# Attention and channel mix in one kernel: the gate by tanh, batch 1 mixed by differences, attention denominators by DVE turns, PSUM banks by name, and a new order of the work

## The chip, the cores and the metric

The kernel runs on one core of a Trainium2 chip. The metric is device time in microseconds (us). A core has five engines with queues of their own: TensorE (PE) for matmuls and transposes into PSUM, VectorE (DVE), ScalarE (ACT), GpSimd (POOL) and SyncE (SP). Here POOL issues the loads, SP the stores, and ACT the first load and the last stores. Before the change the kernel takes 203.44 us, the median of 3 runs (202.97 to 203.64).

## The reference

For each of 8 batches and 8 heads, with 576 tokens, heads of 64 and 32 memory slots:

```python
a = exp(phi - max(phi, axis=2)); a = a / sum(a, axis=2)      # over the tokens
k_m = einsum('bhsm,bhsd->bhmd', a, k); v_m = einsum('bhsm,bhsd->bhmd', a, v)
attn = softmax(scale * q @ k_m.T)                            # over 32 slots
x = (attn @ v_m), heads side by side                         # 8 x 576 x 512
xk = mu_k * x + (1 - mu_k) * x_prev; xr = mu_r * x + (1 - mu_r) * x_prev
k = relu(xk @ w_k); v = (k * k) @ w_v; r = 1 / (1 + exp(-(xr @ w_r)))
out = r * v
```

x_prev is x one token earlier, with zeros ahead of the first. The channel mix has 1024 inner channels. Outputs are float32; inside, most tiles are bfloat16.

## The kernel before, in words

The order of all work is written out in PLAN, a list of words. A word `2:x0` is step x0 of batch 2; `c1:5` is block 5 of the keys of token chunk 1; `g:7` is the gate of token tile 7; `o:7` its value product and store; `sg:3` settles the gates of tiles 6 and 7; `p:` words issue loads. Each engine goes through its own instructions in this order and waits where a semaphore tells it to. A step that waits therefore holds up all that stands behind it on its engine.

A batch's attention goes through these steps:
- `exp` (ACT): the exponential of phi. `z` (PE, L246, then a reciprocal on DVE): its sums. `kv`, or `k` and `v` apart (PE, L236): the sums over the tokens, 72 small matmuls that run several at a time in parts of the array.
- `nk` or `ak`: K scaled by 1/sum, on DVE or ACT. `tk`: turned by PE, copied from PSUM. `q0`, `q1`: q turned on DVE (L323). `s`: scores on PE (L338) and their exponentials on ACT (L343).
- The denominators of the second softmax come in one of two ways. By PE: `l0` to `l3` (L353) sum the 32 slots by a matmul with ones, ACT takes the logarithm (L358) and the exponential of its negative (`h.z`, `r.z`, L363). By turns: `fe` turns the exponentials on DVE, `fs` sums and inverts them, `fo` turns the result back. Batches 0, 1 and 3 go by PE, the others by turns.
- `y` or `w` (DVE, L387): weights times inverse denominators.
- The values and the mixing with the token before also come in two ways. By PE: `nk0` ... `nr1` scale V by 1/sum and by mu or 1 - mu, and `mk0`, `mk1`, `mr0`, `mr1` (L292) add both products in PSUM; ACT and DVE copy xk and xr out (L450). By differences: `x0`, `x1` (L292, copied by ACT, L399) give x, `dd` subtracts the token before on DVE (L411), `k0d` ... `r2e` scale the difference by mu - 1 on DVE or ACT (L424, L422) and add x on DVE (L425). Batches 0 and 1 are mixed by PE, the others by differences.

The channel mix works on chunks of tokens: chunk 0 is batch 0 in two halves (320 and 256 tokens), the others have 512 tokens. A key block is 4 matmuls (L526), a Relu on ACT (L531) and a square on DVE (L540). A gate is 4 matmuls (L556) and exp(-x) on ACT (L561); settling takes the logarithm of 1 + that and the exponential of its negative, for two tiles at once (L567, L568). A value product is 8 matmuls (L582), a product with the gate on DVE (L584), and stores.

Matmuls on a tile of zeros whose result nobody reads (`busy`, L192) stand at two places at the start, 16 of 512 columns.

POOL loads q, k, v and phi of a batch, batch 0 by halves of 64 partitions, and the weights wk, wr, wv in parts; the loads turn float32 into bfloat16, but for phi. PSUM has eight banks, used in turn by one tag with eight buffers.

Of the kernel before, what the change touches and what calls it, by code (L numbers as in the profile page):

```python
# [19 lines left out]
    "0:busy10 0:exp1 0:mub 0:exp0 p:k:0b 0:k0c 0:z 0:hn0 0:k1c p:q:0a 0:ht0 p:q:0b 0:hn1 p:v:0b 0:hc1 0:qh0 0:qh1",  # L20
    "p:v:0a 0:s0 0:l1 0:h1z 0:l0 0:mu 0:s1 0:y1 0:v1c 0:v0c 0:nk1 p:wk:0-4 0:nr0 p:wr:0-4 p:wk:4-8 0:nk0 0:l3 0:h0z",
    "0:y0 0:l2 0:h3z 0:h2z 0:busy6 0:y3 0:y2 0:nr1 0:mr1 0:mk0 g:3 0:mk1 c0:2a 0:mr0 c0:0a p:phi:1 1:exp 7:load p:k:1",
    "c0:4a c0:1a g:2 c0:0b c0:6a 1:z c0:5a p:q:1 c0:1b 1:k 1:nk sg:1 g:0 6:load 1:q0 1:tk 1:q1 c0:4b c0:5b g:1 c0:7b",
    "c0:2b 1:s p:v:1 c0:7a c0:3b c0:3a c0:6b 1:l2 1:v 1:nk1 1:nr1 1:nk0 p:wv:0-2 1:l1 1:l3 1:nr0 1:h2z 1:h1z 1:l0",
    "1:y2 1:y1 1:h3z p:wv:2-4 0:load 1:load 1:y3 1:h0z 1:y0 o:2a o:3a 1:mk1 1:mk0 1:mr0 2:exp c1:5 c1:0 c1:7 1:mr1",
    "c1:3 2:z c1:1 c1:4 o:3b sg:0 2:kv 2:nk o:2b 2:tk 2:q0 2:q1 c1:2 c1:6 o:1b 2:s 2:nv o:1a 3:exp 2:fe g:5 g:4 2:fs",
    "2:fo 2:w0 3:z sg:2 2:w1 o:0b o:4 o:5 2:x0 3:kv 3:nk g:7 3:nv 3:q0 2:x1 g:6 2:load 3:tk 3:q1 2:dd o:0a sg:3 2:k0d",
    "g:8 3:s 4:exp 2:k2d o:6 o:7 3:l1 3:l3 3:l2 2:r0d 3:l0 c2:4 3:r0z 3:w0 3:r1z 3:w1 c2:1 c2:3 3:load c2:0 c2:7 c2:2",
    "4:z 2:r2d 3:x1 4:q0 c2:5 c2:6 3:x0 4:kv 3:dd 4:q1 4:ak 3:k2d g:9 sg:4 o:8 4:tk o:9 3:k0d 4:av 5:exp g:12 g:11",
    "g:10 5:z 4:s 3:r2d 5:kv 3:r0d 4:fe 5:q0 sg:5 c3:2 5:q1 c3:1 c3:7 4:fs 5:av c3:5 g:13 4:fo 5:load 4:load c3:6",  # L30
    "4:w0 7:exp 4:w1 5:ak c3:4 c3:3 o:10 sg:6 o:11 c3:0 7:q1 4:x1 g:14 g:15 7:z 4:x0 sg:7 7:q0 5:tk 4:dd o:12 o:15",
    "6:exp 7:kv 7:ak 5:s 7:av 4:k2d 4:k0d o:14 5:fe 7:tk 4:r2e 6:z o:13 5:fs c4:3 4:r0e 5:fo c4:4 5:w1 c4:5 6:kv 7:s",
    "6:av 6:ak 5:w0 6:q1 6:q0 c4:6 c4:1 g:19 7:fe c4:2 g:16 g:17 5:x0 c4:0 6:tk c4:7 7:fs 5:x1 sg:8 5:dd g:18 sg:9",
    "o:17 5:k0d 5:k2d 6:s o:16 o:19 o:18 5:r2e 5:r0e c5:5 6:fe c5:1 g:21 c5:2 g:20 6:fs c5:0 6:fo sg:10 6:w0 6:w1",
    "c5:3 g:23 c5:4 c5:6 g:22 c5:7 7:fo 6:x1 o:20 7:w0 7:w1 6:x0 sg:11 6:dd o:21 o:22 7:x0 g:25 6:k0d g:24 6:k2d 7:x1",
    "sg:12 7:dd o:23 7:k0d g:26 7:k2d c6:0 6:r0e c6:1 c6:4 6:r2e c6:7 c6:3 c6:5 c6:2 c6:6 c7:4 7:r0e c7:2 c7:7 c7:3",
    "g:27 7:r2e c7:6 c7:0 sg:13 c7:1 o:26 o:25 c7:5 o:27 g:29 o:24 c8:1 c8:4 g:31 g:28 c8:3 sg:14 c8:6 c8:7 g:30 c8:5",
    "o:28 o:29 sg:15 c8:2 o:30 o:31 c8:0 g:33 g:32 sg:16 g:35 g:34 o:33 o:32 sg:17 o:34 o:35",
# [4 lines left out]
SUMS = ()  # L43


NJ = 9


@with_exitstack
def kernel(  # L50
# [13 lines left out]
    nc = tc.nc  # L64
# [18 lines left out]
    ld = ctx.enter_context(tc.sbuf_pool(name="ld", bufs=2))  # L83
    work = ctx.enter_context(tc.sbuf_pool(name="work", bufs=2))
    psum = ctx.enter_context(tc.psum_pool(name="psum", bufs=1))


# [14 lines left out]
    def load_phi(b, eng):  # L102
        ph = ld.tile([128, HH, NJ, M], F32, name="ph", tag="ph")
        eng.dma_start(out=ph.rearrange("p h j m -> p h (j m)"), in_=rows(phi[b]))
        loads[b] = ph
# [25 lines left out]
    nc.scalar.preload_act_table_set("natural_log_exp_and_others")  # L131
# [9 lines left out]
    def preload(word):  # L141
# [6 lines left out]
        elif what == "id":  # L148
            make_identity(nc, identity)
        else:  # L150
            n = int(part[0])
            if what == "phi":
                load_phi(n, nc.gpsimd)
            else:
                dst = qs[n].rearrange("p (h j) d -> p h j d", j=NJ) if what == "q" else kvs[n][:, "kv".index(what)]
                src = {"q": q, "k": k, "v": v}[what][n]
                if n:
                    load_rows(dst, src)
                else:
                    load_parity(dst, src, ROWS["ab".index(part[1])])  # L160

    for word in PRE.split():
        preload(word)

# [23 lines left out]
    def keep_busy(n, blocks=CT // 128):  # L188

        ps = psum.tile([128, CT], F32, name="idle", tag="ps", bufs=8)[:, :blocks * 128]  # L190
# [5 lines left out]
    def load_mu_b():  # L196
        ps = psum.tile([128, 2, 2, D], F32, name="mub", tag="ps", bufs=8)
# [7 lines left out]
    def load_mu():  # L205
        ps_mu = psum.tile([128, 2 * ND], F32, name="psmu", tag="ps", bufs=8)
        nc.tensor.transpose(ps_mu, mu2, ident_f)
        nc.vector.tensor_scalar_add(mu1, ps_mu, -1.0)

    def attention(b):  # L210
        st = {}

        def ps_tile(shape, dtype, name):
            return psum.tile(shape, dtype, name=name, tag="ps", bufs=8)
# [27 lines left out]
        def esum():  # L242
            st["zps"] = ps_tile([128, 2], F32, "zps")
            parts = [em[:, j].rearrange("p h m -> p (h m)") for j in range(NJ)] if b not in SUMS else st["es"]
            for i, part in enumerate(parts):
                nc.tensor.matmul(st["zps"], lhsT=part, rhs=ones, start=i == 0, stop=i == len(parts) - 1,  # L246
                                 skip_group_check=True)
            st["rz"] = work.tile([128, 2], F32, name="rz", tag="rz", bufs=3)
            nc.vector.reciprocal(st["rz"], st["zps"])

        def sum_rows():

            left = work.tile([128, HH * M], F32, name="es", tag="es", bufs=1)
            nc.vector.reduce_sum(left, em.rearrange("p j h m -> p (h m) j"), axis=mybir.AxisListType.X)
            terms = work.tile([128, 3, HH * M], BF16, name="et", tag="et", bufs=1)
            for i in range(3):
                nc.vector.tensor_copy(terms[:, i], left)
                if i < 2:
                    nc.vector.tensor_sub(left, left, terms[:, i])
            st["es"] = [terms[:, i] for i in range(3)]  # L260

        def norm_k(cs=(0, 1), by_act=False):

            def go():
                if "kbd" not in st:
                    st["kbd"] = work.tile([128, 2, 2, 2, PB], BF16, name="kbd", tag="kbd", bufs=3)
# [9 lines left out]
        def norm_v(by_act=False):  # L276

            def go():
                vb = work.tile([128, 2, D], BF16, name="vb", tag="vb", bufs=3)
# [19 lines left out]
        def tr_k(cs=(0, 1), copy=nc.vector.tensor_copy):  # L299

            def go():
# [6 lines left out]
                if "kmT" not in st:  # L308
                    st["kmT"] = work.tile([128, 2, 128], BF16, name="kmT", tag="kmT", bufs=3)
# [3 lines left out]
        def q_tile():  # L313
            if "qT" not in st:
                st["qT"] = work.tile([128, HH, NJ * PB, 2], BF16, name="qT", tag="qT", bufs=2)
# [10 lines left out]
        def scores(cs):  # L326

            def go():
                if "e" not in st:
                    st["e"] = work.tile([128, 2, S], BF16, name="e", tag="e", bufs=3)  # L330
# [15 lines left out]
        def denom(c, hf, by_dve=False):  # L346

            def go():
                if "lz" not in st:
                    st["lz"] = work.tile([128, 2, S], F32, name="lz", tag="lz", bufs=2)  # L350
# [15 lines left out]
        def fold_e():  # L366
            eT = work.tile([128, 2 * NJ, M, 2], BF16, name="eT", tag="eT", bufs=1)
            nc.vector.transpose(eT.rearrange("p b m h -> p (b m h)").bitcast(U32),
                                st["e"].rearrange("p c s -> p (c s)").bitcast(U32))
# [269 lines left out]
```

## Time and profile before

| | |
|---|---|
| median of 3 runs | 203.44 us |
| span of the profiled execution | 201.9 us |
| mean granted PE clock | 0.975 |
| busy: PE, DVE, ACT, POOL | 191.1, 147.1, 156.9, 29.3 us |
| matmuls: keys, values, gates | 352, 328, 144 |
| settling the gates on ACT | 19.4 + 19.0 us |
| squares of the keys on DVE | 31.4 us |
| DMA moved | 31.29 MB, mean 155 GB/s |

The result file holds no time of the profiled execution itself beside its span; the span runs from its first to its last instruction, so what lies around it is the difference from the times, 1.5 us from the median.

A profile line gives an engine's line in the kernel, the operation, the tile written and those read, the shape and the count, the busy us and the mean ns of one, and the idle time ahead of it with what ended that. In the row of slices, each digit is the busy share of 5 us in tenths. A line of a timeline gives the start, the length of a merged run of equal instructions, and in brackets the engine's wait before it. Busy times of matmuls overlap, so times on PE are best read from one start to the next.

### The profile page before, as it was taken

Reading aid. Unit: us, or ns where it says so; the run is one execution under the profiler, and the core shown is the slowest. Engines: PE = TensorE matmul, PEld = TensorE weight load, DVE = VectorE, ACT = ScalarE, POOL = GpSimd, SP = SyncE. Lnnn points to the kernel's source line nnn. Section 1 sums busy time; section 2 is a strip of 40 time slices with the busy share of each in tenths; the row PEclk is TensorE's granted clock in tenths of the full one; section 3 lists DMA queues with packets and bytes.
Section 4 is the critical chain, followed back from the end, with each engine's and each line's share of the span. In section 5 each row is a group of like instructions: output and inputs, shape, how many; then the busy total and the mean of one; then the engine's idle time right before and its main releaser. Section 6 shows DMA issues by size and latency. Waiting matters only on the chain.

```text
span 201.9 us, 5395 instructions
## 1 busy us (share of the span) xinstructions
PE 191.1 (95%) x2179; PEld 98.4 (49%) x2179; DVE 147.1 (73%) x347; ACT 156.9 (78%) x313; POOL 29.3 (15%) x45
## 2 busy tenths in 40 slices
PE   8459999899999999999999999999999999999992
PEld 2324576546654445544456654444444444444451
DVE  2366566967898989999699979998998835243231
ACT  3146899787858989899896999988999992592760
POOL 7743412212204100045000000000000000000000
PEclk9856999999999999999999999999999999999999
DMA  6999999999999999989999200520242004404435
GB/s 161 167 204 209 264 208 198 265 223 270 222 265 258 236 311 210 288 149 205 247 247 271 66 3 17 123 67 3 65 95 54 3 0 107 101 0 107 104 71 136
DMA packets 24521, 31.29 MB, mean 155 GB/s; under 512 B 1960, under 2 KB 19632, under 8 KB 24496
## 3 DMA queue, kind: packets, MB, share of 16 engines
q0 software_dynamic: 17392, 20.91, 55.6%
q1 hardware_dynamic: 6336, 9.18, 17.4%
q10 hardware_dynamic: 768, 0.85, 1.3%
q8 instruction: 17, 0.28, 0.5%
q14 instruction: 8, 0.07, 0.1%
HBM read 38.28 MB, written 9.44 MB: 236 GB/s over the span
## 4 chain that ended last, share of the span: by engine, by line
PE 90%; DMA 4%; ACT 2%; DVE 1%; POOL 1%; issue 1%; POOLq 0%
PE pk L526 31%; PE pv L582 30%; PE pr L556 16%; DMA q<-in_q_dram 4%; PE kvps L236 4%; PE scps L338 2%; PE mxps L292 2%; PE nops L292 2%; PE idle L192 1%; PE zps L353 1%; PE zps L246 1%; DVE qT L323 1%; POOL kv L111 1%; ACT lz L358 0%; ACT lz L363 0%
## 5 line engine op out<-in xcount | busy, mean ns | idle before, releaser
L526 PE MATMUL pk<-xkT,wk 128*128 128x512 bf16 (+4 forms) x352 | 67.9, 341 | 0.0
L582 PE MATMUL pv<-wv,sq 128*128 128x512 bf16 (+1 forms) x328 | 66.4, 353 | 0.4 <-ACT lz L358 0.4
L531 ACT ACTIVATE rl<-pk 128x512 bf16<-128x512 f32 (+3 forms) x80 | 41.4, 566 | 13.7 <-PE pk L526 12.8
L526 PEld LDWEIGHTS <-wk 128*128 128x128 bf16 x352 | 32.9, 98 | 28.7 <-issue 0.8
L582 PEld LDWEIGHTS <-sq 128*128 128x128 bf16 x328 | 31.1, 98 | 30.3 <-issue 0.8
L540 DVE TENSOR_TENSOR sq<-rl 128x512 bf16<-128x512 bf16 (+5 forms) x104 | 31.4, 334 | 19.2 <-ACT rl L531 18.7
L556 PE MATMUL pr<-wr,xrT 128*128 128x512 bf16 x144 | 35.4, 379 | 0.5 <-ACT xrT L450 0.5
L584 DVE TENSOR_TENSOR o<-sg,pv 128x512 f32<-128x512 f32 (+1 forms) x41 | 24.6, 617 | 13.3 <-PE pv L582 13.1
L561 ACT ACTIVATE sg<-pr 128x512 f32<-128x512 f32 x36 | 21.4, 610 | 5.6 <-PE pr L556 4.8
L556 PEld LDWEIGHTS <-xrT 128*128 128x128 bf16 x144 | 13.4, 98 | 15.2 <-ACT xrT L450 0.6
L567 ACT ACTIVATE sg<-sg 128x1024 f32<-128x1024 f32 x18 | 19.4, 1079 | 0.2
L568 ACT ACTIVATE sg<-sg 128x1024 f32<-128x1024 f32 x18 | 19.0, 1058 | 0.6
L399 ACT CAST x<-nops 128x320 bf16<-128x320 f32 (+1 forms) x48 | 15.7, 426 | 3.2 <-PE nops L292 3.2
L323 DVE STREAM_TRANSPOSE qT<-q 128x576 uint32<-128x576 uint32 (+1 forms) x16 | 13.3, 839 | 2.2 <-DMA q<-in_q_dram 2.1
L387 DVE TENSOR_TENSOR atn<-e,lz 128x576 bf16<-128x576 bf16 (+2 forms) x20 | 12.1, 633 | 1.1 <-ACT lz L363 0.7
L343 ACT ACTIVATE e<-scps 128x288 bf16<-128x288 f32 x32 | 10.6, 416 | 2.5 <-PE scps L338 2.3
L422 ACT ACTIVATE mu_d<-diff,mu 128x576 bf16<-128x576 bf16 x16 | 11.6, 797 | 0.2 <-DVE xkT L425 0.2
L224 ACT ACTIVATE em<-ph 128x1152 bf16<-128x1152 f32 (+1 forms) x9 | 9.4, 1060 | 2.6 <-DMA ph<-in_phi_dram 2.6
L425 DVE TENSOR_TENSOR xrT<-x,mu_d 128x1152 bf16<-128x1152 bf16 x12 | 9.1, 755 | 3.2 <-ACT mu_d L422 3.0
L236 PE MATMUL kvps<-kv,em 64*32 64x128 bf16 (+1 forms) x720 | 8.8, 217 | 2.1 <-DMA kv<-in_k_dram 2.1
L424 DVE TENSOR_SCALAR mu_d<-diff,mu 128x576 bf16<-128x576 bf16 x32 | 10.2, 363 | 0.0
L108 POOL DMA_DIRECT2D kv<-in_k_dram x7 | 5.2, 746 | 32.1 <-PE kvps L236 26.4
(66 smaller groups left out, 152.6 us busy)
## 6 DMA issues: line engine op xcount, KB each, us to landing
out_dram<-o SPq DMA_DIRECT2D x61, 128.0 KB, 2.4
ph<-in_phi_dram POOLq DMA_DIRECT2D x7, 576.0 KB, 19.5
kv<-in_k_dram POOLq DMA_DIRECT2D x7, 576.0 KB, 18.7
q<-in_q_dram POOLq DMA_DIRECT2D x7, 576.0 KB, 21.2
kv<-in_v_dram POOLq DMA_DIRECT2D x7, 576.0 KB, 20.8
out_dram<-o SPq DMA_DIRECT2D x18, 64.0 KB, 5.3
wk<-in_moe_w_k_dram POOLq DMA_DIRECT2D x2, 512.0 KB, 13.6
wv<-in_moe_w_v_dram POOLq DMA_DIRECT2D x2, 512.0 KB, 20.5
```

The source lines that it names most:

```text
L236: nc.tensor.matmul(kvps[c][g * M:(g + 1) * M], lhsT=em[ROWS[c], j, g, :], rhs=kv5[ROWS[c], parts, g, j, :], start=j == 0, stop=j == NJ - 1 ...
L323: nc.vector.transpose(dst.bitcast(U32), src.bitcast(U32))
L399: nc.scalar.copy(st["x"][:, i, sl], pss[i])
L526: nc.tensor.matmul(pk[:, p0 - lo:p1 - lo], lhsT=wk_sb[:, di, fi * 128:(fi + 1) * 128], rhs=xk_T[:, di, p0 % RING:p0 % RING + p1 - p0], sta ...
L531: nc.scalar.activation(rl, pk, AF.Relu)
L540: nc.vector.tensor_mul(sq[:, fi, p:p + p1 - p0], rl[:, part], rl[:, part])
L556: nc.tensor.matmul(pr, lhsT=xr_T[:, di, c0:c0 + 128], rhs=wr_sb[:, di, :], start=(di == 0), stop=(di == ND - 1))
L561: nc.scalar.activation(sg[:, t % 2], pr, AF.Exp, scale=-1.0)
L567: nc.scalar.activation(gated[p], gated[p], AF.Ln, bias=1.0)
L568: nc.scalar.activation(gated[p], gated[p], AF.Exp, scale=-1.0)
L582: nc.tensor.matmul(pv[:, cols], lhsT=sq[:, fi, p:p + 128], rhs=wv_sb[:, fi, cols], start=(fi == 0), stop=(fi == NF - 1))
L584: nc.vector.tensor_mul(o[:, cols], gated[t // 2][:, t % 2, cols], pv[:, cols])
```

## The change

It has these parts:
- The gate: r = 1/(1 + exp(-z)) becomes (1 + tanh(z/2))/2. ACT does one Tanh for a tile, settling goes, and DVE's product becomes (tanh + 1) times the value in one scalar_tensor_tensor. The half is put into the keys: Relu scales by the root of 1/2. The instruction list shows a second load of an ACT table ahead of the first Tanh; the first load stands behind the issue of the first K load.
- Squares of the keys: 41 instructions of them go to ACT (blocks with an s), the rest stay on DVE.
- Batch 1 is mixed by differences; batch 0 still by PE. In several batches `x0m`, `x1m` split the values' copies between ACT and DVE, and differences and mixing go by pairs of tiles.
- Denominators: all batches from 1 on go by turns, in whole, in halves (`fe0`) or in quarters (`qe1`); batch 0 has one quarter by turns and three by PE.
- Loads: batch 0's q by pairs of heads, all partitions at once; batch 0's v in one; batch 1's phi and half of its q stand ahead of the weights; every later load is a word of its own in the plan.
- PSUM: each tile takes the bank that a string names, in the plan's order. Other buffers have names of their own; gates have four tiles of one token tile each.
- Unread matmuls: 76, of 128 to 512 columns (198 blocks of 128 in all), at 18 places of the start.
- The plan is in another order throughout; batch 2's K and V sums stand apart in it.

The core of the diff:

```diff
-    "0:busy10 0:exp1 0:mub 0:exp0 p:k:0b 0:k0c 0:z 0:hn0 0:k1c p:q:0a 0:ht0 p:q:0b 0:hn1 p:v:0b 0:hc1 0:qh0 0:qh1",
-    "p:v:0a 0:s0 0:l1 0:h1z 0:l0 0:mu 0:s1 0:y1 0:v1c 0:v0c 0:nk1 p:wk:0-4 0:nr0 p:wr:0-4 p:wk:4-8 0:nk0 0:l3 0:h0z",
...
+    "0:busy4x2 0:busy2x1 p:k:0b 0:busy3x4 0:exp1 0:exp0 0:busy9x4 0:busy3x3 0:busy11x3 0:mub p:q:00 0:busy4x3 0:z 0:k",
+    "p:q:01 0:busy4x3 0:ak 0:q0 0:q1 0:busy1x2 p:v:0 0:ta 0:busy4x3 0:busy1x3 0:s0 0:s1 0:busy6x4 0:qe1 0:l3 0:v1c",
+    "0:nk1 0:l0 p:phi:1 0:h3z 0:qs1 0:v0c 0:busy1x1 0:qo1 0:l2 0:nr0 p:q:11 0:mu 0:h2z 0:y1 0:h0z 0:nk0 0:y2 0:y3",
+    "0:y0 0:busy13x1 0:busy1x3 0:busy2x2 1:exp 0:nr1 0:busy5x2 0:mk1 1:z 0:mk0 p:wk:0-4 0:busy2x1 0:mr0 p:k:1 c0:1as",
+    "c0:2a c0:0bs c0:3a c0:3b 1:q1 c0:2bs 1:k c0:1b 0:mr1 1:nk p:wk:4-8 p:q:10 c0:0as c0:7b 1:q0 c0:7a 1:ta c0:4a",
+    "c0:5b 1:s0 p:wr:0-4 1:qe0 1:s1 1:fe1 1:qe1 1:fs1 c0:6a c0:4bs 1:fo1 1:fs0 1:y2 1:qo0 g:3 g:2 p:v:1 c0:6b c0:5as",
+    "1:v 1:av g:0 g:1 1:y0 1:y3 1:qo1 1:x0 p:wv:2-4 1:y1 o:1b 1:x1m 1:d0d p:wv:0-2 1:d2d o:2b p:phi:2 o:0b o:3a p:k:2",
+    "1:k0e 1:k2e 1:r0d o:2a o:0a 2:exp o:3b c1:5 c1:3 2:z 2:k 2:nk 1:r2d p:q:2 p:v:2 c1:2s 2:q1 c1:1s 2:q0 2:tk c1:7s",
...
+    banks = iter(BANKS)
+
+    def bank():
+        return f"ps{next(banks)}"
...
-        def fold_e():
-            eT = work.tile([128, 2 * NJ, M, 2], BF16, name="eT", tag="eT", bufs=1)
-            nc.vector.transpose(eT.rearrange("p b m h -> p (b m h)").bitcast(U32),
-                                st["e"].rearrange("p c s -> p (c s)").bitcast(U32))
+        def fold_e(b0, n):
+            def go():
...
+                nc.vector.transpose(
+                    st["eT"][:, b0:b0 + n].rearrange("p b m h -> p (b m h)").bitcast(U32),
+                    st["e"].rearrange("p c s -> p (c s)")[:, b0 * 64:(b0 + n) * 64].bitcast(U32))
...
-                    nc.scalar.copy(st["x"][:, i, sl], pss[i])
+                    (nc.vector.tensor_copy if both and i % 2 else nc.scalar.copy)(st["x"][:, i, sl], pss[i])
...
+                nc.scalar.activation(rl, pk, AF.Relu, scale=HALF_ROOT)
...
+                    if by_act:
+                        nc.scalar.activation(sq[:, fi, p:p + p1 - p0], rl[:, part], AF.Square)
...
-            nc.scalar.activation(sg[:, t % 2], pr, AF.Exp, scale=-1.0)
...
-            nc.scalar.activation(gated[p], gated[p], AF.Ln, bias=1.0)
-            nc.scalar.activation(gated[p], gated[p], AF.Exp, scale=-1.0)
+            nc.scalar.activation(gated[t], pr, AF.Tanh, scale=0.5)
...
-                nc.vector.tensor_mul(o[:, cols], gated[t // 2][:, t % 2, cols], pv[:, cols])
+                nc.vector.scalar_tensor_tensor(o[:, cols], in0=gated[t][:, cols], scalar=1.0, in1=pv[:, cols],
+                                               op0=AL.add, op1=AL.mult)
```

## The prediction

> **What bounds the kernel now.** I read the page's first two parts, then the stretches of 5 us, then the order of time on TensorE (PE) and GpSimd (POOL), and last the groups by line.
>
> ```profile
> PE 191.1 (95%) x2179; PEld 98.4 (49%) x2179; DVE 147.1 (73%) x347; ACT 156.9 (78%) x313; POOL 29.3 (15%) x45
> PE   8459999899999999999999999999999999999992
> PEclk9856999999999999999999999999999999999999
> DMA  6999999999999999989999200520242004404435
> ```
>
> PE is full from the fourth slice to the last but one; VectorE (DVE) and ScalarE (ACT) have room on average. The holes lie at the start, where the DMA row is full, and in the end.
>
> ```profile
> 5.00:10.00 5.00, 2.55 (x88) 2.00 (x87) 1.57 (x6) 0.87 (x2) 3.59 (x5) 0.81 1.11 166
> 10.00:15.00 5.00, 2.62 (x49) 1.09 (x53) 3.41 (x5) 2.16 (x7) 2.22 (x3) 0.50 1.21 204
> 15.00:20.00 5.00, 4.58 (x120) 2.45 (x112) 3.38 (x10) 3.10 (x11) 1.76 (x2) 0.66 1.24 206
> 20.00:25.00 5.00, 4.94 (x65) 2.72 (x66) 3.08 (x9) 4.05 (x10) 1.85 (x3) 1.00 1.17 267
> 149.54 10.36 PE pk L526 x48
> ```
>
> The columns are busy us of PE, weight loads, DVE, ACT and POOL, then granted clock, DMA share, GB/s. Until 20 us PE is half idle at half clock while about 200 GB/s come in; from 20 us it is full at clock 1.00. The last line, of the chain of waits, shows the dense rate: 10.36 us / 48 = 216 ns for a 512-column matmul. Three things alone can move the end, therefore: fewer matmuls after 20 us, the moment when dense work begins and keeps on, and the tail behind the last matmul (last starts near 198, span 201.9).
>
> The span is 201.9 us; the median of the runs shown is 203.44. I take 1.5 us as lying around the span and add it at the end.
>
> **Matmuls taken away or added after 20 us.**
>
> ```profile
> 35.86 1.92 PE L582 MATMUL pv<-wv,sq 128*128 128x256 bf16 x16 [0.45 <-ACT lz L358]
> 37.71 2.18 PE L292 MATMUL mxps<-atn,vm 32*64 32x256 bf16 x64
> 42.51 0.42 PE L292 MATMUL mxps<-atn,vm 32*64 32x256 bf16 x16
> 58.75 0.34 PE L292 MATMUL nops<-atn,vb 32*64 32x320 bf16 x8
> 34.20 0.75 PE L236 MATMUL kvps<-kv,em 64*32 64x64 bf16 x72
> ```
>
> I count from a group's start to the next group's start, since ends overlap.
> - Batch 1's mixing by PE (80 matmuls) goes: 37.71 to 39.82 and 42.51 to 42.87, 2.46 us. Two halves of plain values come instead: batch 2's took 0.27 (58.75 to 59.02) and 0.25. Net -1.9.
> - Denominators: batch 1's four sums on PE, 0.23 and 0.37 of pure work, and batch 3's four, 67.87 to 68.36, 0.49. Net -1.1. Batch 0 loses one of four, inside the waiting start: 0.
> - The pause before 35.86: 0.6 us in which the first value product waited for half of wv (landed 35.81). The new order puts these products later, -0.6, while other waits come (next part).
> - Batch 2's K and V sums stand apart: twice 0.68 (34.20 to 34.88) for one of 0.74. +0.6.
>
> Together -3.0. Everything else on PE (352 key, 144 gate, 328 value matmuls) is the same in count and width.
>
> **The start.** POOL issues loads with at most eight on the way; they land in order, and the queue is never empty.
>
> ```profile
> 8.90 0.75 POOL L104 DMA_DIRECT2D ph<-in_phi_dram  x1 [0.89 <-DMA kv<-in_k_dram]
> 13.69 0.74 POOL L108 DMA_DIRECT2D kv<-in_v_dram  x1 [0.68 <-DMA kv<-in_v_dram]
> 17.67 0.87 POOL L147 DMA_DIRECT2D wv<-in_moe_w_v_dram  x1 [1.25 <-DMA wk<-in_moe_w_k_dram]
> ```
>
> Each line was issued 0.3 us behind a landing: k's second half 8.6, v's first half 13.4, wk's first half 17.4. The trace's landings give the rest: q 10.5 and 12.0, v 15.2, wr 19.9, wk 22.6, phi of batch 1 24.1, k 26.8, q 29.6, v 33.1, wv 35.8 and 38.5. So a half load takes 1.65, phi 1.56, a full one 2.7 to 3.5, a weight 2.1 to 2.7. The new order (k, q, v of batch 0; phi and half of q of batch 1; wk; k; wk; half of q; wr; v; wv) lands by these: v 15.2, phi 16.8, half q 18.4, wk 20.4, k 23.1, wk 25.7, half q 27.2, wr 29.8, v 33.0, wv 35.7 and 38.4. The total to wv is the same, so it ends the same.
>
> Batch 0's chain in the new order: q at 12.0, DVE turn 0.76, scores from 12.8, four exponentials to 14.5. Then PE meets the added wait: V's sums stand ahead of the second denominator and need all of v (15.2); behind them are queued the denominators, and for these ACT's logarithm and exponential (0.38 to 0.47 each, six) and DVE's products (0.42, 0.49), to 18.7. Mixing, evacuated by 20.6. The first key block so starts at 20.7, by its rows and by wk (20.4) alike. In the trace dense work begins with the gate at 20.06 and the keys at 21.37. No gain, no loss.
>
> From 20.7 PE has, until chunk 1's keys: 64 key matmuls of 320 columns and 64 of 256 (136 and 109 ns apart) 7.8, batch 1's K and V 1.4, transposes and scores 0.7, the rest of batch 0's mixing 0.9, four gates 3.5, batch 1's values 0.6 and exits 0.3, seven half value products of 8 x 109 ns 6.1: 21.3. Ahead of wk's second half stand 5.0 us of this work, so PE comes to it at 25.7, as it lands; then it waits for the turn of q (27.2 + 0.76) 0.2, for wr 0.3, for v 0.4: 0.9. So chunk 1 starts at 42.9. The trace has it at 39.82, but with two half products made instead of seven (4.4) and one mixing half open (0.36): the same work stands at 44.6. That is -1.7, and it holds the items above except batch 3's sums (-0.5) and batch 2's (+0.6). The sum is **-1.6: span 200.3**, and with the 1.5 around it **201.8 us**.
>
> **The unread matmuls** are 198 blocks of 128 columns. At 216 ns per 512 that is 10.7 us; the trace's first ten ran 427 ns apart, which would make 21. Those ahead of K's sums are 112 blocks: half rate to about 4.7, then full as in the trace (clock 1.00 up to 8 us), they end near 9, and K's second half lands at 8.6. Later ones lie in waits for q, exponentials and products. What hides them is the loads: at full clock they cost nothing, at half clock 3 us.
>
> **Off the path.** Settling goes from ACT, 19.4 + 19.0 us:
>
> ```profile
> L567 ACT ACTIVATE sg<-sg 128x1024 f32<-128x1024 f32 x18 | 19.4, 1079 | 0.2
> L568 ACT ACTIVATE sg<-sg 128x1024 f32<-128x1024 f32 x18 | 19.0, 1058 | 0.6
> L433 DVE SCALAR_TENSOR_TENSOR vm<-kvps,rz,mu_m 128x128 bf16<-128x128 f32 x8 | 2.4, 346 | 0.5 <-PE kvps L236 0.4
> L584 DVE TENSOR_TENSOR o<-sg,pv 128x512 f32<-128x512 f32 x31 | 20.5, 682 | 11.9 <-PE pv L582 11.8
> ```
>
> ACT gets 41 squares. No row shows one; the exponentials from and to SBUF (0.42 at 256 columns, 0.47 at 320, 0.68 at 576) give 0.62 at 512, 21 us in all; the ends are DVE's 0.41 and the scaling's 0.80. With 12 more scalings (0.80) and fewer logarithms and copies ACT falls by some 16 us. DVE loses 41 squares (14 us by L540's 0.18 to 0.41) and 5 us of scalings of K and V now on ACT or gone. It gains 2.2 batches of turns at 3.87 (L368, L374, L375, L380: 0.77 + 1.35 + 0.38 + 1.37) and 36 more pieces at 0.1, 12; 18 copies of x (0.42 to 0.48) for 8 of the mixing, 4; and batch 1's differences and additions with their pairs, 7: about +4. Tanh is taken to last as the exponential of the same size (0.61), between its closest spacing (0.49) and the 1024-column exponential (1.08). So neither overtakes PE, and their slack buys nothing, since PE did not wait for them from 40 us on. The tail stays: the last product (0.42) starts at 197.96, 0.45 behind PE and not behind ACT's last settling (195.2), and its store ends the span, 3.9 us behind PE, on the same SP and ACT queues. Later loads are issued in another order on POOL; in the trace batch 2's k, v and q landed at 42.8, 46.4 and 49.2. In the new order (k, q, v) the uses come at 44.9 (chunk 1's start, two blocks and one sum later), some 50 and 50.5, 1 us or more behind each landing: nothing, unless POOL's wait for a free buffer grows by more.
>
> A second table load stands before the first Tanh, in this stretch; the trace has one of 1.28 us. ACT has about that much room between 20 and 36 us. The Trainium skill (ScalarE: Activation LUTs, "What ACT_TABLE_LOAD costs") puts a switch with its drain at about 2.66 us; by that, chunk 1 starts up to 1.4 later, and the span would be 201.7 at most; no run so far shows a switch in mid-kernel.
>
> The product with the gate becomes a scalar_tensor_tensor. L433, with one operand in PSUM and one in SBUF too, took 346 ns at 128 columns, where a tensor_scalar took 345. I add nothing; at worst it doubles (a rival).
>
> **Rivals.**
> 1. *Slower: batch 1's differences come late.* Before chunk 1 stand, one behind the other: the values' evacuation, differences (0.9 a pair), two scalings a pair on ACT (1.33 dense), an addition (0.68). From the second values at 37.5: 38.3, 39.2, 40.6, 41.9, 42.7. That is 0.2 ahead of PE's need, and ACT's backlog (table load, squares) lies ahead of it. Each us beyond 42.9 is a us of the end: at 44.5 the gain is gone, from 45.1 on it is slower. Two us late: span 202.3; three: 203.3, 204.8 us. For it: ACT is the fullest engine there; against it: the old mixing needed copies too.
> 2. *Better: no new waits.* If loads land 1 us sooner, the 0.9 us go: span 199.4, 200.9 us; if chunk 0 starts sooner as well, some 200. The order of arrivals speaks for it, the full DMA row against it.
> 3. *The product takes twice as long on DVE*: 31 x 0.68 + 10 x 0.42 = 25 us more; between 60 and 160 us DVE is 93% busy, so PE would wait some 6 us: 208 us. The Trainium skill (Vector Engine (DVE) Microarchitecture Reference, "Points that are easy to get wrong") says that this instruction halves its rate with two SBUF sources that are not bf16; here one is in PSUM, and L433 speaks against it. 3%.
> 4. *The fillers do not keep the clock up*: K's sums 3 us late, chunk 0 at some 23, +2.5: 204.3 us. 3%.
>
> **Numbers.** Forecast (200.9 to 202.8) 45%; better 19%; differences late by 1.2 to 2.2 us 18% (within 0.3%, about what a measurement of this kernel can tell from no change); later still 12%, with 3 and 4 slower 18%. So faster 0.64, same 0.18, slower 0.18. The range 199.8 to 204.6 leaves out the ends of 2 and 1.
>
> **What would show it.** PE clock 1.00 from 5 us on; wk's first half near 20.4 and the first key there; PE idle 0.9 us between 25 and 36; chunk 1 at 43; from there no idle PE and the same tail of 3.9 us. An ACT that is full up to 42 us with PE idle behind it is rival 1. What makes the forecast wrong: loads that do not keep the trace's pace in the new order, or hidden waits on PE after 45 us.

## The result, and the profile after

The changed kernel takes 204.32 us (median of 16 runs, 203.26 to 206.19), beside it the kernel before 203.66 (16 runs, 202.83 to 204.15). The ratio is 1.0034, 95% interval 1.0019 to 1.0049: slower by 0.3%, where the prediction had 201.8 us and faster. The time lies inside the range, the sign is wrong. The profiled execution has a span of 202.5 us, with 1.8 around it.

From the page of the changed kernel, the rows that answer to those of before: busy time by engine, PE's slices, granted clock, the instruction queue (packets, MB, share), and the chain that ended last.

```profile
PE 194.4 (96%) x2236; PEld 101.8 (50%) x2236; DVE 148.3 (73%) x385; ACT 143.0 (71%) x310; POOL 29.8 (15%) x45
PE   8998999999999999699999999999999999999992
PEclk9999999999999999999999999999999999999999
q8 instruction: 17, 0.28, 0.5%
PE 93%; ACT 2%; issue 2%; DVE 1%
```

The clock is full throughout, PE is even fuller than before, ACT has lost 13.9 us: much went as forecast. But PE's slices now have one hole, a 6 in the slice of 81 to 86 us, where the kernel before had none, and the chain has 2% "issue" (1% before), time in which the engine waited for nothing that the profile shows. First the waits of PE (who waited for what: us in total, times, longest us), then its order of time in that stretch and at two other places (start, length of the run of equal instructions, count, and in brackets the wait ahead of it):

```profile
PE pv L612 <- issue: 1.9, 1, 1.9
PE kvps L266 <- issue: 1.1, 2, 0.8
PE idle L213 <- DVE zeros L143: 1.0, 1, 1.0
```

```profile
82.14 0.37 PE L275 MATMUL zps<-ones,em 128*128 128x2 bf16 x9
82.44 0.48 PE L356 MATMUL scps<-qT,kmT 32*32 32x288 bf16 x32
82.85 0.84 PE L266 MATMUL kvps<-kv,em 64*32 64x128 bf16 x72
85.55 1.89 PE L612 MATMUL pv<-wv,sq 128*128 128x512 bf16 x8 [1.85 <-issue]
...
16.65 0.35 PE L266 MATMUL kvps<-kv,em 64*32 64x64 bf16 x23 [0.79 <-issue]
...
51.47 0.54 PE L266 MATMUL kvps<-kv,em 64*32 64x64 bf16 x47 [0.35 <-issue]
```

In the kernel before, the list of PE's waits has no "issue"; it names a load or another engine each time, the longest first:

```profile
PE kvps L236 <- DMA kv<-in_k_dram: 2.1, 2, 1.2
PE scps L338 <- DVE qT L323: 1.3, 1, 1.3
```

In the changed kernel it holds only "issue", beside the wait for the first zeros. Two stand in the midst of a run of equal sums (of 36 and of 72 matmuls) that has begun already and writes the banks that it holds. Counted from start to start, PE stands from 83.47, the last of batch 5's 72 sums, to 85.55, 2.08 us.

**What lies at these places.** The 17 packets of the instruction queue are 16 KB each. Each matmul is two instructions of PE (weight load and matmul). Numbered in the program's own list, the instructions that came late are 443, 699, 1211, 1723 and 2747: all the same modulo 256 (187). So I take a packet for a page of 256 instructions (64 bytes each), and each late one for the first of a page. For each page boundary the trace gives the packet's start:

| page entered | packet for the next page starts | PE reaches its end | next page's first matmul | PE stands | packet to first |
|---|---|---|---|---|---|
| 10.68 | 14.29 | 15.67 | 16.65 | 0.98 | 2.36 |
| 16.65 | 20.34 | 22.21 | 22.57 | 0.36 | 2.23 |
| 28.73 | 32.16 | 34.14 | 34.42 | 0.28 | 2.26 |
| 45.27 | 49.09 | 50.91 | 51.47 | 0.56 | 2.38 |
| 79.43 | 83.26 | 83.47 | 85.55 | 2.08 | 2.29 |

In the kernel before, the packet always started 3.15 us or more ahead of the page's first matmul, and PE has no such wait. So the theory: **PE waits for its instructions**, 2.2 to 2.4 us behind a packet's start, where a page of many small matmuls passes quickly. In the last row of the table the page holds batch 4's sums and scores and batch 5's 72 sums, and ends with them.

The rivals: (O) the new order itself costs the time, through a hidden dependency at these steps; (B) as one form of it, the value product at 85.55 waits for its PSUM bank, which the scores of batch 4 used before. The chain of waits of the profile tells it in that way:

```profile
82.51 0.52 PE scps L356 x23
83.03 1.32 ACT e L361 x4
84.35 1.20 issue
85.55 1.89 PE pv L612 x8
```

Even there 1.20 us remain behind ACT's last exponential that nothing explains.

### The profile page after: what moved, and what is told of

Its sections match the earlier page's. It is cut to its first block, busy times and chain, and to the rows that moved or that the text cites. A ratio compares the mean times of both kernels' runs of the same rounds, so it can differ in the third digit from the quotient of the medians.

```text
span 202.5 us, 5537 instructions
## 1 busy us (share of the span) xinstructions
PE 194.4 (96%) x2236; PEld 101.8 (50%) x2236; DVE 148.3 (73%) x385; ACT 143.0 (71%) x310; POOL 29.8 (15%) x45
## 4 chain that ended last, share of the span: by engine, by line
PE 93%; ACT 2%; issue 2%; DVE 1%
PE pv L612 31%; PE pk L562 30%; PE pr L595 16%; PE idle L213 6%; PE kvps L266 4%; PE nops L310 2%; PE scps L356 2%; PE zps L275 1%; PE mxps L310 1%; ACT e L361 1%; DVE atn L416 1%; ACT rl L566 1%; PE ktps L323 0%; DVE qT L341 0%; PE zps L371 0%
## 5 line engine op out<-in xcount | busy, mean ns | idle before, releaser
L566 ACT ACTIVATE rl<-pk 128x512 bf16<-128x512 f32 (+3 forms) x80 | 41.7, 557 | 12.9 <-PE pk L562 9.7
L614 DVE SCALAR_TENSOR_TENSOR o<-sg,pv 128x512 f32<-128x512 f32 (+1 forms) x41 | 24.7, 612 | 23.0 <-PE pv L612 21.5
L574 DVE TENSOR_TENSOR sq<-rl 128x512 bf16<-128x512 bf16 (+5 forms) x63 | 18.4, 324 | 12.3 <-ACT rl L566 12.2
L451 ACT ACTIVATE mu_d<-diff,mu 128x576 bf16<-128x576 bf16 x28 | 20.1, 783 | 1.9 <-DVE xkT L454 1.1
L572 ACT ACTIVATE sq<-rl 128x512 bf16<-128x512 bf16 (+5 forms) x41 | 20.1, 509 | 1.1
L428 ACT CAST x<-nops 128x320 bf16<-128x320 f32 (+1 forms) x38 | 12.9, 426 | 4.1 <-PE nops L310 4.1
L213 PE MATMUL idle<-zeros 128*128 128x384 bf16 (+3 forms) x76 | 14.4, 343 | 1.0 <-DVE zeros L143 1.0
L416 DVE TENSOR_TENSOR atn<-e,lz 128x256 bf16<-128x256 bf16 (+2 forms) x29 | 12.8, 477 | 0.2
L440 DVE TENSOR_TENSOR diff<-x 128x512 bf16<-128x512 bf16 (+1 forms) x42 | 12.3, 349 | 0.2
L341 DVE STREAM_TRANSPOSE qT<-q 128x576 uint32<-128x576 uint32 x16 | 11.9, 758 | 0.0
L407 DVE STREAM_TRANSPOSE lz<-se 128x576 f32<-128x576 f32 (+3 forms) x19 | 11.3, 613 | 0.1
L454 DVE TENSOR_TENSOR xkT<-x,mu_d 128x1152 bf16<-128x1152 bf16 x14 | 10.5, 753 | 0.6 <-ACT mu_d L451 0.3
L266 PE MATMUL kvps<-kv,em 64*32 64x64 bf16 (+1 forms) x792 | 9.5, 207 | 1.2 <-issue 1.1
```

The lines of the kernel that those rows point to most:

```text
L213: nc.tensor.matmul(ps.rearrange("p (a b) -> p a b", b=128), lhsT=zeros, rhs=zeros.unsqueeze(1).to_broadcast([128, blocks, 128]), start=Tru ...
L266: nc.tensor.matmul(kvps[c][g * M:(g + 1) * M], lhsT=em[ROWS[c], j, g, :], rhs=kv5[ROWS[c], parts, g, j, :], start=j == 0, stop=j == NJ - 1 ...
L416: nc.vector.tensor_mul(st["at"][:, c, sl], st["e"][:, c, sl], st["lz"][:, c, sl])
L451: nc.scalar.activation(t[:, i], st["d"][:, pr + i, :], AF.Copy, scale=mu1[:, o:o + 1])
L566: nc.scalar.activation(rl, pk, AF.Relu, scale=HALF_ROOT)
L572: nc.scalar.activation(sq[:, fi, p:p + p1 - p0], rl[:, part], AF.Square)
```

## The experiments

Each ratio is to the kernel before, measured beside it; spans are those of the profiled executions, and the shifts are in instructions. "Chunk 1" is the start of the first key block of 512 columns that is followed by batch 2's sums; "last" is the last matmul's start.

| kernel | span | chunk 1 | last | ratio to before, 95% interval |
|---|---|---|---|---|
| before | 201.9 | 43.97 | 197.65 | 1 |
| changed | 202.5 | 43.14 | 198.43 | 1.0034 (1.0019 to 1.0049) |
| shift 98 | 204.0 | 44.78 | 199.90 | 1.0071 (1.0052 to 1.0091) |
| shift 130 | 202.0 | 43.91 | 197.88 | 1.0001 (0.9983 to 1.0019) |
| sums moved apart | 201.6 | 44.02 | 197.47 | 0.9956 (0.9932 to 0.9980) |
| shift -48 | 200.8 | 43.40 | 196.71 | 0.9933 (0.9912 to 0.9954) |
| narrow unread matmuls | 202.7 | 45.10 | 198.54 | 1.0055 (1.0029 to 1.0082) |
| -48, batch 2 apart too | 200.7 | 43.10 | 196.58 | 0.9935 (0.9912 to 0.9959) |
| before, shift 96 | 201.7 | 43.92 | 197.61 | 1.0012 (0.9996 to 1.0029) |
| all squares on DVE | 205.9 | 42.88 | 201.75 | 1.0151 (1.0108 to 1.0195) |
| shift 156 | 200.6 | 43.31 | 196.43 | 0.9948 (0.9926 to 0.9969) |
| before, shift 120 | 202.6 | 44.81 | 198.46 | 1.0005 (0.9987 to 1.0022) |
| shift 156, six short | 200.7 | 43.47 | 196.54 | 0.9954 (0.9933 to 0.9974) |

### Moving the page boundaries: shifts of 98 and 130

Only unread matmuls ahead of 20 us are cut; the plan behind them stays as it is.

```diff
-0:busy9x4 0:busy3x3 0:busy11x3
+0:busy36x1 0:busy3x3 0:busy33x1
```

> Two groups of unread matmuls are issued in narrower pieces over the same columns (9 of 512 columns become 36 of 128, 11 of 384 become 33 of 128), so that PE's stream has 98 instructions more before 20 us and all that follows stands 98 places later against the packets of 256 instructions. Every result is still computed. Theory P1 (PE waits for a packet where a burst of small matmuls stands right ahead of a boundary; from packet to first instruction 2.2 to 2.5 us): the boundary near 83 us moves 98 instructions forward in the work, where only 141 instead of 235 instructions stand in the 2.3 us ahead of it, so the gap there falls from 2.08 us to under 0.3, that at 51 us goes, and the span falls from 202.5 to 199.5 to 200.5, ratio to the kernel before 0.985 to 0.993. Theory P2 (a packet starts only 3.4 to 3.9 us after the page before it was entered, so that no page of 256 instructions passes in under about 6.0 us, wherever its burst lies): the page that holds the burst of 81 to 84 us still has about 1.8 us to wait, those near 19 and 25 us wait 1.4 each (in part hidden by the waits for loads), span 202 to 204. Theory O (the order itself costs the time, the packets nothing): unchanged, 202.5, with the gap of 2 us at the same instruction.

The shift of 130 has this besides:

```diff
-p:q:00 0:busy4x3 ... p:q:01 0:busy4x3
+p:q:00 0:busy12x1 ... p:q:01 0:busy12x1
```

> As the kernel shifted by 98, and two more groups of 4 unread matmuls of 384 columns become 12 of 128: 130 instructions more than the changed kernel. P1: no gap near 83 us, but one near 100 us, where 246 instructions stand in the 2.3 us ahead of a boundary: 1.5 to 2.3 us; span 201.5 to 202.5. P2: 1.8 us near 82 and 3.1 near 100 us, span 203.5 to 205.5, slower than the changed kernel. O: unchanged, 202.5.

The order of time on PE near 84 us, first with the shift of 98, then with 130:

```profile
84.27 0.36 PE L266 MATMUL kvps<-kv,em 64*32 64x128 bf16 x23
85.83 0.60 PE L266 MATMUL kvps<-kv,em 64*32 64x128 bf16 x49 [1.20 <-issue]
86.37 1.90 PE L612 MATMUL pv<-wv,sq 128*128 128x512 bf16 x8
```

```profile
83.25 0.25 PE L266 MATMUL kvps<-kv,em 64*32 64x128 bf16 x7
84.32 0.74 PE L266 MATMUL kvps<-kv,em 64*32 64x128 bf16 x65 [0.83 <-issue]
84.99 1.90 PE L612 MATMUL pv<-wv,sq 128*128 128x512 bf16 x8
```

This is the clearest reading of the study. In the changed kernel PE stood behind all 72 sums. With 98 instructions more it stands 49 sums earlier, with 130 more 65 earlier: half the count of instructions each time, a matmul being two. A dependency belongs to a step and would have stayed with it; this wait stays with a place in the instruction stream. And the value product follows its sums without a wait, in the same bank and behind the same exponentials. That rules out O and B for this gap. (The shift of 130 has two more waits of this kind, 1.00 at 12.9 and 1.05 at 25.0 us.)

Where along a burst a boundary falls was not what I first thought, though. That only the burst right ahead of a boundary counts (P1) fails: the shift of 98 still has 1.42 us here (84.41 to 85.83), and 0.83 and 0.98 at 19.9 and 104.7. P2 has it near 84 (1.8 forecast), but its 3.1 near 100 us with the shift of 130 did not come at all; there the page lasted only 3.2 us, and its packet had started 1.2 us before the page ahead was entered. P1's gap near 100 us did not come there either. The shift of 98 is also slower as a whole: chunk 1 starts 1.6 us later than in the changed kernel. In its profiled execution the granted clock was at half from 21.6 to 25.0 us:

```profile
PEclk9999699999999999999999999999999999999998
```

Whether that is the reason is not shown. Its five other executions list a mean clock of 0.998 to 1.000 and took about as long (205.2 to 205.9 us, the profiled one 205.8), though such a mean misses stretches without a clock record (see the narrow unread matmuls below). With the shift of 130, whose pieces are as narrow, the clock stayed full.

### The burst broken up

```diff
-5:kv 4:fe0 o:11 4:fs
+o:11 5:kv 4:fe0 4:fs
```

> The value step of token tile 11 (8 matmuls of 512 columns, 1.9 us) moves ahead of the sums of batch 5 (144 small matmuls), with its PSUM bank exchanged with one of theirs; the count of instructions ahead of the boundary near 83 us changes by 16 only and the same page holds 1.9 us more work. P1 and P2 alike: the gap of 2.08 us at 83.5 us falls to 0.2 to 0.5, the others stay, span 200.6 to 201.0, ratio to the kernel before about 0.994. O: a step that runs earlier by 0.9 us and sums that run later by 1.9 change nothing or cost a little: 202.5 or more, the gap still there.

PE near 84 us:

```profile
83.03 0.48 PE L356 MATMUL scps<-qT,kmT 32*32 32x288 bf16 x32
83.45 1.90 PE L612 MATMUL pv<-wv,sq 128*128 128x512 bf16 x8
85.28 1.05 PE L266 MATMUL kvps<-kv,em 64*32 64x128 bf16 x72
86.26 1.90 PE L562 MATMUL pk<-xkT,wk 128*128 128x512 bf16 x8
```

1.9 us of work more lie in the same page, which again takes 6.06 us (80.02 to 86.08), and of the 2.08 us 0.29 are left, inside the sums. The span falls by 0.9 instead of 1.7, because chunk 1 starts 0.88 later than in the changed kernel; in this profiled execution the clock was at half from 17.5 to 20.9 us. Behind chunk 1 it gains 1.8.

### A shift the other way, by -48

```diff
-0:busy4x2 0:busy2x1 ... 0:busy3x3 0:busy11x3 ... 0:busy13x1 ... 0:busy2x2 ... 0:busy5x2
+0:busy2x4 0:busy1x2 ... 0:busy2x4 0:busy8x4 ... 0:busy3x4 ... 0:busy1x4 ... 0:busy3x4
```

(three groups of 4 of 384 columns become 3 of 512, and one of 2 of 128 becomes 1 of 256 likewise.)

> Ten groups of unread matmuls are issued in wider pieces (13 of 128 columns become 3 of 512, 11 of 384 become 8 of 512, and so on), about the same columns: PE's stream has 48 instructions less before 36 us than in the changed kernel. P1: the gap at 83 us goes (39 instructions ahead of that boundary), one of 0.5 to 1.0 near 50 us stays: span 200.3 to 201. P2: the same there (the page that ends near 82 us holds more long work), 1.3 near 28 us in place of the 0.3 near 34, 0.6 near 51: span 200.5 to 201.5, ratio to the kernel before 0.990 to 0.997. O: unchanged, 202.5.

```profile
PE kvps L266 <- issue: 1.1, 2, 0.9
PE idle L213 <- DVE zeros L143: 1.0, 1, 1.0
```

```profile
83.03 0.84 PE L266 MATMUL kvps<-kv,em 64*32 64x128 bf16 x72
83.81 1.90 PE L612 MATMUL pv<-wv,sq 128*128 128x512 bf16 x8
```

The same plan, the same banks, the same real matmuls: the value product follows the sums at once, the wait of 1.9 us is gone, and the kernel is 0.7% faster than before and 1.0% faster than the changed one by the two ratios (0.9933 / 1.0034). It beats both. The gain lies behind chunk 1, where the real work is the same: from there to the last matmul's start this kernel takes 153.3 us and the changed one 155.3, while chunk 1 itself starts 0.26 later here. So it does not come from the wider unread matmuls. P2's wait near 28 us did not come, the one at 51 was 0.42, and 1.10 stand at 16.2 us, which neither P1 nor P2 had.

### Batch 2's gap taken away as well

On the kernel shifted by -48, one key block moves ahead of batch 2's V sums; two entries of the string of banks are exchanged likewise.

```diff
-c1:6 o:1a 2:s 2:v ... p:phi:3 2:fs0 c1:4s c1:0s
+c1:6 o:1a 2:s c1:4s 2:v ... p:phi:3 2:fs0 c1:0s
```

> On the kernel shifted by minus 48, one key block of chunk 1 (8 matmuls of 512 columns with their banks, 1.9 us) moves from behind batch 2's V sums to ahead of them, so that the page of instructions that ends there (entered at 45.81, next at 51.91, a gap of 0.43 at 51.48) holds 1.9 us more work. Packet theory: that gap goes, the rest stays: span 200.2 to 200.6 against 200.8, ratio to the kernel before about 0.991. Order theory: no change, or batch 2's values and mixing come later and PE waits.

First the kernel shifted by -48, then this one:

```profile
51.05 0.63 PE L266 MATMUL kvps<-kv,em 64*32 64x64 bf16 x49
51.91 0.28 PE L266 MATMUL kvps<-kv,em 64*32 64x64 bf16 x23 [0.23 <-issue]
```

```profile
51.03 1.02 PE L562 MATMUL pk<-xkT,wk 128*128 128x512 bf16 x3 [0.20 <-ACT rl L566]
51.99 0.91 PE L266 MATMUL kvps<-kv,em 64*32 64x64 bf16 x72
```

The gap inside the sums is gone and nothing is gained: the key block, now earlier, waits for its bank until ACT has done the Relu of the block before, and of the 0.30 that this run was ahead at chunk 1 only 0.13 are left at the last matmul.

### The same in the order of before

```diff
-0:busy10 ... 0:busy6
+0:busy40x1 ... 0:busy24x1
```

> The kernel before, in which the 10 unread matmuls of 512 columns become 40 of 128 and the 6 become 24: the same columns, 60 instructions more before 5 us and 96 more from 22 us on. Packet theory: boundaries that in the kernel before fell where a page lasted 6.1 us or more now end pages of 4.4 to 4.8 us: up to 1.3 us of waiting near 34, 1.5 near 88 and 1.7 near 118 us, less what PE's stream has run ahead; span 203 to 205 against 201.9, with gaps marked issue in the midst of the small sums. If packets matter only in the changed order: 201.9, no new gap.

No gap and no change (1.0012, 0.9996 to 1.0029): a miss. Three pages there lasted 4.5 to 5.0 us, and PE did not wait, since their packets started between 0.1 and 2.3 us behind the entry of the page ahead, not 3.7. In the tail of every run, among long matmuls only, the packet for the last page that PE enters starts 2.4 to 4.8 us before the page ahead of it is entered; where that entry lies in a burst of sums, packets start up to 4.4 us behind it. From this I made a reckoning, which no run shows directly: PE's instruction reader runs ahead of the matmuls, loses that lead in a burst, and asks for the next page about 3.7 us behind its own entry into one. Put through the order of each kernel, it gave 3.7 us of waits for the changed kernel (about 4.0 measured) and none for the kernel before and for its shift by 96. The next two runs tested it.

### Shift by 156, and before by 120

Seven groups of unread matmuls are cut into pieces of 128 or 256 columns:

```diff
-0:busy4x2 ... 0:busy3x4 ... 0:busy9x4 0:busy3x3 0:busy11x3 ... p:q:00 0:busy4x3 ... p:q:01 0:busy4x3
+0:busy8x1 ... 0:busy12x1 ... 0:busy36x1 0:busy9x1 0:busy33x1 ... p:q:00 0:busy12x1 ... p:q:01 0:busy6x2
```

> The changed kernel with 156 instructions more ahead of 15 us: seven groups of unread matmuls in pieces of 128 or 256 columns over the same columns. The packet theory as the eight runs so far leave it: PE's instruction reader runs at most some 40 instructions ahead of the matmuls and has no lead behind a burst of small ones; the packet for the next page starts about 3.7 us after the reader enters a page, and 2.3 us later the next page can begin. Put through the order of the changed kernel this gives 3.7 us of waits for it (measured about 4.0), and for this shift no wait above 0.15 anywhere: no gap marked issue, span 199.3 to 200.3 if the granted clock holds as in the run shifted by 130, ratio to the kernel before 0.984 to 0.991. Order theory: 202.5. If only less narrow pieces matter: as with the shift by 98, 204.

```diff
-0:busy10 ... 0:busy6
+0:busy52x1 ... 0:busy24x1
```

> The kernel before with 120 instructions more (10 unread matmuls of 512 columns become 52 of 128, 12 of these additional, and 6 become 24). By the same reckoning, which gives no wait for the kernel before and none for its shift by 96 (as measured), a boundary now lies where batch sums follow each other near 113.5 us: one gap of 0.8 to 1.2 us there, none elsewhere; span 202.5 to 203.3 against 201.9, ratio 1.003 to 1.008. If hidden waits belong to the changed order alone: no gap, 201.7 as with the shift by 96.

PE's waits with "issue" in the shift by 156, all that are left:

```profile
19.36 0.41 PE L310 MATMUL mxps<-atn,vm 32*64 32x256 bf16 x13 [0.59 <-issue]
...
25.28 0.48 PE L266 MATMUL kvps<-kv,em 64*32 64x64 bf16 x40 [0.56 <-issue]
```

Behind 26 us nothing waits, as reckoned. But two waits at the start (0.89 and 0.74 from start to start) were not forecast, and the gain is smaller than expected: the span is 200.6 and the ratio 0.9948, where 0.984 to 0.991 stood. The median of its 11 times is 203.40 us, 1.0 above the profiled execution's 202.39; what the others lose, no profile shows. Nor does the wait in the kernel before come: at 114.41 its packet had started 2.5 us ahead, just early enough. The lead of 40 instructions does not come out of the traces either: a packet that starts 4.5 us ahead of PE's own entry (159.74 and 164.27 in the kernel before) would by the 3.7 need a lead of 8.2 us, some 38 matmuls of 216 ns or 76 instructions, by estimate. So the reckoning is too rough for when a reader with a lead asks for the next page, and that stays open. What every run bears out is the last step: in the 22 cases of all kernels where PE stood 0.25 us or more at a page boundary, the next page began 2.2 to 2.6 us behind its packet's start, and in no other case sooner than 2.2.

### The unread matmuls themselves

On the kernel shifted by -48, every one of them 2 columns wide:

```diff
-nc.tensor.matmul(ps.rearrange("p (a b) -> p a b", b=128), lhsT=zeros,
-                 rhs=zeros.unsqueeze(1).to_broadcast([128, blocks, 128]), start=True, stop=True,
+nc.tensor.matmul(ps[:, :2], lhsT=zeros,
+                 rhs=zeros[:, :2], start=True, stop=True,
```

> On the kernel shifted by minus 48, every unread matmul is 2 columns wide in place of 128 to 512; their count, and so each place in PE's stream, stays. Forecast's step (unread matmuls raise the clock and cost nothing): the granted clock falls to about half in several of the slices between 5 and 20 us, as in the kernel before, batch 0's sums and scores take up to twice as long, first key block at 22 to 24 instead of 21.5 us, span 201.5 to 203.5 against 200.8. Rival (they cost as much as they bring): 200.5 to 201.

The first keys of chunk 0, shifted by -48 and then with the narrow ones:

```profile
22.06 3.12 PE L562 MATMUL pk<-xkT,wk 128*128 128x320 bf16 x24
```

```profile
21.77 5.10 PE L562 MATMUL pk<-xkT,wk 128*128 128x320 bf16 x24
```

The first key comes no later than in the shift by -48, where 22 to 24 us had been expected, but the same 24 matmuls take 2 us longer. One by one, those of 256 columns are 213 ns apart up to 25.80 us and 109 from there on: PE runs at half rate until then. Chunk 1 starts 1.7 us later, the last matmul 1.8. The page's clock row shows 9 in these slices all the same. The trace's first clock record of that run stands at 25.9; where there is none, the row is not to be trusted, but the spacing of equal matmuls is.

The other way, six of the broad ones in front of batch 0's V sums cut to 128 columns, on the shift by 156:

```diff
-0:s1 0:busy6x4 0:qe1
+0:s1 0:busy6x1 0:qe1
```

> As the kernel shifted by 156, with the six unread matmuls of 512 columns near 14 us, in front of batch 0's V sums and denominators, 128 wide instead (the same count). Unread matmuls that hide behind loads cost nothing: same as shifted by 156 within 0.2 us. Rival: they stand in the way of batch 0's mixing, whose first key block comes up to 0.5 sooner without them: 0.2 to 0.5 less; or the clock falls for lack of work: 0.5 to 2 more.

Nothing is gained or lost: 200.7 against 200.6, and chunk 1 0.16 later.

### The squares on ACT

On the kernel shifted by -48, `by_act` is ignored: all 104 squares on DVE.

```diff
-                    if by_act:
+                    if False:
```

> On the kernel shifted by minus 48, all 41 squares that ACT takes go back to DVE: ACT falls by some 20 us to 123, DVE rises by some 14 us (41 of about 0.34) to 162. Forecast's step (slack of ACT and DVE buys nothing): span 200.5 to 201.3. Rival: DVE, 93% busy between 60 and 160 us, becomes the bound there, PE waits for squares and products, span 203 to 207.

The chain that ended last, and the Relu's and squares' groups:

```profile
PE 67%; DVE 26%; ACT 3%; issue 3%; DVEq 0%; ACTq 0%
```

```profile
L566 ACT ACTIVATE rl<-pk 128x512 bf16<-128x512 f32 (+3 forms) x80 | 43.4, 561 | 27.3 <-PE pk L562 15.8 <-DVE sq L574 9.2 <-issue 1.8
L574 DVE TENSOR_TENSOR sq<-rl 128x512 bf16<-128x512 bf16 (+5 forms) x104 | 30.6, 332 | 9.2 <-ACT rl L566 8.8
```

DVE rises by 11 us only, to 159.5 (77% of the span), and yet a quarter of the chain is DVE's: the Relu waits 9.2 us for the buffers that the squares are to free, and PE for the Relu. The rival is right in kind: by the profiled spans it is 5 us slower. Not all of this need be the squares' doing, for the clock was at half for 3.4 us from 114.7 us on, which is worth up to 1.7 us:

```profile
PEclk9999999999999999999999699999999999999999
```

The one execution with a mean clock of 0.998 took 205.24 us, 2.7 more than the median of the shift by -48 (202.55). So the squares cost some 3 to 5 us.

## Why the prediction was wrong, point by point

- **What bounds the kernel: right.** The chain of the kernel after is 93% PE.
- **The net of -3.0 us of matmuls: right, by its sum.** Batch 1's two halves of values take 0.52 from start to start (36.39 to 36.66 and 37.64 to 37.89), for 2.46 of mixing: -1.9, as forecast (in the shift by -48 they take 0.74). Behind chunk 1 the kernel with no page wait (shift 156) needs 153.1 us to its last matmul's start; the prediction's 42.9, 200.3 and 3.9 make 153.5 to the last matmul's end, there 153.4.
- **The start: nearly right.** The prediction counts 64 key matmuls of 320 columns and 64 of 256 for chunk 0; there are 32 of each, and its 7.8 us is the sum for these. wk landed at 19.7 (20.4 forecast), the first keys came at 21.5 (20.7) and chunk 1 at 43.14 (42.9). PE, 0.8 late, found q, wr and v landed, so the 0.9 us of waits for them did not come. The page wait of 0.98 in batch 0's V sums stands ahead of the first keys; how much of the 0.8 is due to it no run separates, since the shifts that remove it wait elsewhere before 26 us.
- **The unread matmuls: right.** Full clock from 5.6 us on, and without their width 1.8 us more; rival 4 was priced at 2.5.
- **Rival 1, differences too late: did not come.** Chunk 1's keys wait for no difference.
- **Tanh, squares, table load, product: right in size.** Tanh takes 595 ns, as the exponential did (610); 41 squares on ACT 20.1 us (21 estimated); ACT fell by 13.9 us (16 forecast) and DVE rose by 1.2 (4 forecast). The product with the gate at 128x512 takes 676 ns against 682 before, at 128x256 414 against 417:

```profile
L614 DVE SCALAR_TENSOR_TENSOR o<-sg,pv 128x512 f32<-128x512 f32 x31 | 20.9, 676 | 21.8 <-PE pv L612 21.1 <-ACT sg L598 0.7
L598 ACT ACTIVATE sg<-pr 128x512 f32<-128x512 f32 x36 | 21.1, 595 | 12.4 <-PE pr L595 12.4
L572 ACT ACTIVATE sq<-rl 128x512 bf16<-128x512 bf16 (+5 forms) x41 | 20.1, 509 | 1.1
```

  So rival 3 falls. The second table load takes 1.28 us from 32.29, where the square before it ends, to the first Tanh at 33.59, as long as the one at the start. The 2.66 of the Trainium skill (ScalarE: Activation LUTs, "What ACT_TABLE_LOAD costs") are not seen here.
- **"Their slack buys nothing, since PE did not wait for them": right as a statement on less work, but not on more.** With the 41 squares back on DVE, DVE has a quarter of the chain and the kernel is slower. The mean of 73% had hidden that.
- **"From there no idle PE": this step failed.** From chunk 1 to the last matmul's end the prediction had 153.5 us, the kernel took 155.6. The difference is the two page waits behind 43 us, 0.56 and 2.08, less some 0.5 by which the rest was quicker. "Hidden waits on PE after 45 us" was named as what would make the forecast wrong, but no rival had it and no price stood beside it. The rest of the gap to 200.3 is 0.2 at chunk 1. That the time still lies inside the range is luck: the range's upper part stood for late differences and the like, and none of these came.
- **What lies around the span** was 1.8 us in place of 1.5, in both kernels measured side by side (203.66 - 201.9): that much of the 204.32 was no effect of the change.

The profile of before could have shown it in part: it names the instruction queue, its packets lie in the trace, and a page entered 3.15 us behind its packet has less than 1 us to spare. The new plan puts sums, scores and sums of two batches (226 instructions) into 1.5 us at 82 us. Where the pages' boundaries fall could be counted from the program.

The Trainium skill (Runtime: NRT & Kernel Launch, "Instruction fetch mechanics") says that instructions are fetched in pages of 256 while the page before runs, and that crossing into the next is mostly hidden. The page size agrees with the packets of 16 KB here; crossing is hidden at 11 of the changed kernel's 16 boundaries whose page came in a packet, and costs 0.28 to 2.08 us at the others.

## What to carry to other kernels

Small matmuls of several steps put side by side fill PE well, but also run through a page of 256 instructions in less time than the next one needs: look for "issue" in the midst of a run of equal matmuls, and count whether the instruction stands where others that waited stand, modulo 256. An extra or a missing unread matmul far ahead moves all boundaries behind it, so two kernels of equal work may differ by 1% for no reason in their plan; before an order is called better or worse, try it with a shift or two. Long matmuls between two bursts, inside the same page, hide the fetch.

## What the hardware showed that I had not expected

- From an instruction packet's start to the first matmul of its page: 2.2 to 2.6 us in every case where PE was waiting for it; the packet itself takes 0.9 to 1.1 us. In 21 of those 22 cases the packet had started 3.0 to 4.3 us behind the entry of the page ahead, so that this page lasted 5.3 to 6.5 us however short its work. In the other (the shift of 130, PE standing from 12.9 us) it started 1.95 us behind, and the page lasted 4.2.
- The granted clock fell to half for 3.4 us at 21.6, 17.5 and 114.7 us in three profiled executions (shift of 98, sums moved apart, all squares on DVE). In each, PE had stood for about 1 us shortly before; in others it stood as long (0.98 and 2.08 us in the changed kernel) and the clock held. No run tells these apart.
- The profile's clock row reads full where the trace holds no clock record, in slices whose 256-column matmuls were 213 ns apart, for 109 at full rate.
